# Transposing q and k by DMA instead of on TensorE, from tile 14 of 36 on, with six output staging buffers and fewer weight buffers

## The chip, the cores and the metric

The kernel runs on one core of a Trainium2 chip. The time is the device time of that core in microseconds, the median of several executions. A profiled execution gives the trace. A difference under about 0.2% can hardly be told from none.

The engines that matter: TensorE (PE) multiplies matrices and also transposes, VectorE (DVE) and ScalarE (ACT) do elementwise work and empty PSUM, GpSimd (POOL) issues the loads here, and SyncE (SP) issues the output stores. Each engine works through its own queue in order.

## The reference

Sliding-window causal attention with a linear bias (ALiBi) over 8 batches, 8 heads, 576 positions and head dimension 64, then a gated feed-forward layer over the 4608 tokens.

```python
scores = scale * np.matmul(q, k.transpose(0, 1, 3, 2))        # [8, 8, 576, 576]
mask = (rel >= 0) & (rel < 128)                               # rel = i - j
scores = np.where(mask, scores + slopes * -abs(rel), -1e9)
attn = softmax(scores)
x = np.matmul(attn, v)                                        # to [4608, 512]
g = x @ w_gate                                                # [512, 1536]
out = (g * sigmoid(g) * (x @ w_val)) @ w_out                  # [4608, 512], float32
```

## The kernel before

**Tiles.** The 4608 tokens are cut into 36 tiles of 128, numbered 0 to 35 in the order of loading (the code calls the number `rank`). Two batches make a pair `s` of nine tiles: four full tiles of each batch, and tile 4 of the pair (ranks 4, 13, 22, 31), which combines the last 64 rows of both. `source` gives where a tile lies in HBM.

**Loads.** POOL loads q, k and v of a tile (`qn`, `kn`, `va`) and turns float32 into float16 on the way. `qn` and `kn` have four buffers each, `va` has fourteen places.

**Transposes.** The scores need q and k with the head dimension on the partitions: `qT` and `kT`, one buffer for a pair `s`, two buffers in all. `transposed` makes them: four 128x128 transposes on PE into a PSUM tile `pt` (line 162) and one copy by DVE into `qT` or `kT` (line 163). That is eight transposes and two copies for a tile.

**Attention.** Unit `i` of 36 takes 128 keys. `scores` multiplies them with 256 queries into PSUM (`ps`, line 221; `psc`, line 192, for the combined tile), ACT takes the exponent (`exr`, `exrc`), DVE multiplies with a constant mask that holds the bias (`ex`; `exl` for the last full tile of a batch, which the combined tile needs again; `exc` for the combined tile). `weighted` multiplies with v (`av`) and divides by the sum, which gives `x`. `x_transposed` brings x onto the partitions (`px`, `xT`). The PSUM pool `ps_a` with four banks serves `pt`, `ps`, `psc`, `av` and `px`.

**Feed-forward.** Nine blocks `n` of 512 tokens. `gate_val` makes `pg` (line 302) and `pv` (line 312), ACT and DVE make `hT` from them; `project` multiplies with `w_out` into `po` (line 326), ACT scales it into the staging buffer `osb` (line 330), and SP stores that (line 332). The projection of block n-1 runs between the parts of block n.

**Order.** One function emits both: after every step of the feed-forward, as many attention steps follow as a rate (`RATE`) asks for, and at least those that the next block needs. `attention` transposes what unit i+1 needs, computes its scores, then the weighted sum of unit i, then it loads tile i+7 and calls `ahead`. `ahead` transposes what unit i+4 needs, but only where the tile's number reaches `QK_DMA_FROM`; at 99 it does nothing. A scheduler then orders the instructions within each engine, so that the written order is not the order on the queues, and it sets the waits.

Of the kernel before, what the change touches and what calls it, by code (L numbers as in the profile page):

```python
# [10 lines left out]
FP16 = mybir.dt.float16  # L11
# [3 lines left out]

P = 128
WIN = 128
QK_DMA_FROM = 99
X_DMA_FROM = 99
FIRST = 4  # L20
RATE = 5.2
# [20 lines left out]
def kernel(  # L42
# [11 lines left out]
    B, H, S, D = q.shape  # L54
# [46 lines left out]
    epool = ctx.enter_context(tc.tile_pool(name="ep", bufs=3))  # L101
# [1 line left out]
    bpool = ctx.enter_context(tc.tile_pool(name="bp", bufs=3))  # L103
    hpool = ctx.enter_context(tc.tile_pool(name="hp", bufs=18))
    supool = ctx.enter_context(tc.tile_pool(name="sup", bufs=4))
    opool = ctx.enter_context(tc.tile_pool(name="op", bufs=3))
    ps_f = ctx.enter_context(tc.tile_pool(name="ps_f", bufs=3, space=PSUM))
    ps_a = ctx.enter_context(tc.tile_pool(name="ps_a", bufs=4, space=PSUM))

# [15 lines left out]
    def col_of(p):  # L125
        return p if p < 4 else (p + 1 if p < 8 else 4)
# [38 lines left out]
    def transposes(rank):  # L165
        s, c = divmod(rank, 9)
        if s not in qTs:
            qTs[s] = tpool.tile([P, 4, 9 * P], FP16, name="qT", tag="qT")
            kTs[s] = tpool.tile([P, 4, 9 * P], FP16, name="kT", tag="kT")
        if rank >= QK_DMA_FROM:  # L170
            cols = slice(c * P, (c + 1) * P)
# [9 lines left out]
    def scores(i):  # L181

        s, p = units[i]
        c = col_of(p)
        kcols = slice(c * P, (c + 1) * P)
        kT, qT = kTs[s], qTs[s]
        if p == 8:
            banks = [ps_a.tile([P, 4, P], FP32, name="psc", tag="a") for _ in range(2)]
            for j in range(4):
                for par in range(2):  # L190
                    rows = slice(64 * par, 64 * par + 64)
                    nc.tensor.matmul(banks[par][:, j, :], kT[rows, j, kcols], qT[rows, j, kcols],
                                     start=(j == 0), stop=(j == 3))
            er = epool.tile([P, H, P], FP16, name="exrc", tag="exrc", bufs=2)
            e = epool.tile([P, H, P], FP16, name="exc", tag="exc", bufs=2)
            ex[(s, p)] = e

            er4 = er.rearrange("k (a par b) q -> k a par b q", a=2, par=2)

            def act(par):  # L200
                nc.scalar.activation(er4[:, :, par], banks[par].rearrange("k (a b) q -> k a b q", a=2),
                                     AF.Exp, scale=scale)

            return [[lambda: act(0)],
                    [lambda: act(1), lambda: nc.vector.tensor_mul(e, er, com)], [], []]

        banks = []
        for q4 in range(2):
            two = [ps_a.tile([P, 2, 256], FP32, name="ps", tag="a") for _ in range(2)]
            banks.append(two)  # L210
            for j in range(2):
                pair = 2 * q4 + j
                if p == 7:
                    parts = [(0, slice(8 * P, 9 * P)), (P, slice(4 * P, 5 * P))]
                else:
                    parts = [(0, slice(c * P, (c + 2) * P))]
                for n, (o, cols) in enumerate(parts):
                    w = cols.stop - cols.start
                    for par in range(2):
                        rows = slice(64 * par, 64 * par + 64)  # L220
                        nc.tensor.matmul(two[par][:, j, o:o + w], kT[rows, pair, kcols],  # L221
                                         qT[rows, pair, cols],
                                         start=(j == 0 and n == 0),
                                         stop=(j == 1 and n == len(parts) - 1))
        er = epool.tile([P, H, 256], FP16, name="exr", tag="exr", bufs=2)
        if p in (3, 7):
            e = epool.tile([P, H, 256], FP16, name="exl", tag="exl", bufs=3)
        else:
            e = epool.tile([P, H, 256], FP16, name="ex", tag="ex", bufs=3)
        ex[(s, p)] = e  # L230
        m = lo if p == 3 else hi if p == 7 else reg

        def act(q4, par):
            o = 4 * q4 + 2 * par
            nc.scalar.activation(er[:, o:o + 2, :], banks[q4][par], AF.Exp, scale=scale)  # L235

        def mul(q4):
            o = slice(4 * q4, 4 * q4 + 4)
            nc.vector.tensor_mul(e[:, o, :], er[:, o, :], m[:, o, :])  # L239

        return [[lambda: act(0, 0)], [lambda: act(0, 1), lambda: mul(0)],
                [lambda: act(1, 0)], [lambda: act(1, 1), lambda: mul(1)]]
# [112 lines left out]
    def transposes_to(r):  # L355
        nonlocal done_t
        while done_t <= min(r, NR - 1):
            transposes(done_t)
            done_t += 1

    def ahead(i):

        r = min(need_rank[min(i + 4, last)], loaded - 1)
        if r >= QK_DMA_FROM:
            transposes_to(r)

    def attention():

        transposes_to(need_rank[0])
        for steps in scores(0):  # L370
            for f in steps:
                f()
        yield 0
        for i in range(last + 1):
            after = [[], [], [], []]
            if i < last and i != FIRST - 1:
                transposes_to(need_rank[i + 1])
                after = scores(i + 1)
            if i == 1:
                make_lo()  # L380
            if i == 5:
                make_hi()
                make_com()
            for fs in after:
                for f in fs:
                    f()
                yield i
            weighted(i)
            yield i
            if i >= FIRST:  # L390
                loads_to(i + 7)
                ahead(i)
            yield i
            x_transposed(i)
            yield i
            yield i + 1
            if i == FIRST - 1:

                transposes_to(need_rank[i + 1])
                for fs in scores(i + 1):  # L400
                    for f in fs:
                        f()
                    yield i + 1
# [79 lines left out]
```

## Time and profile before

| | |
|---|---|
| median of 3 runs | 387.88 us (387.79 to 388.63) |
| profiled execution | 388.84 us, span 387.1 us |
| granted TensorE clock | 0.998 |
| PE transposes of q and k | 288 matmuls (line 162), 72 copies on DVE (line 163) |
| output stores | 40 on SP's queue, 2.0 us to landing for a full tile |
| loads of a q, k or v tile | 4.8, 4.5 and 5.9 us to landing (median) |

In the lines of the profile a group's row reads: line, engine, operation, output<-inputs, shapes, count | busy us, mean ns of one | idle time of that engine just before, and what ended it. A row of the timeline begins with the start and the length in us. A row by stage gives start:end, length, and for each engine the busy us and the number of instructions, then the granted clock, the DMA share and GB/s. A wait's row gives who waited for whom: us in total, times, the longest. A row of an issue ends with the median us from issue to landing. SPq and POOLq are those engines' own issuing queues.

### The profile page before, as it was taken

Reading aid. Unit: us, or ns where it says so; the run is one execution under the profiler, and the core shown is the slowest. Engines: PE = TensorE matmul, PEld = TensorE weight load, DVE = VectorE, ACT = ScalarE, POOL = GpSimd, SP = SyncE. Lnnn points to the kernel's source line nnn. Section 1 sums busy time; section 2 is a strip of 40 time slices with the busy share of each in tenths; the row PEclk is TensorE's granted clock in tenths of the full one; section 3 lists DMA queues with packets and bytes.
Section 4 is the critical chain, followed back from the end, with each engine's and each line's share of the span. In section 5 each row is a group of like instructions: output and inputs, shape, how many; then the busy total and the mean of one; then the engine's idle time right before and its main releaser. Section 6 shows DMA issues by size and latency. Waiting matters only on the chain.

```text
span 387.1 us, 6587 instructions
## 1 busy us (share of the span) xinstructions
PE 365.6 (94%) x2592; PEld 181.1 (47%) x2592; DVE 250.2 (65%) x515; ACT 173.8 (45%) x317; POOL 108.7 (28%) x134
## 2 busy tenths in 40 slices
PE   1889899999999999999999999999999999999994
PEld 1454345545545455554454544545454444444441
DVE  3765798757976598558865687668843752753540
ACT  1552474455544554545654456454633323332321
POOL 8966648842422055225200531000000000000000
PEclk9999999999999999999999999999999999999999
DMA  9999999999897369599441956310011001001013
GB/s 143 141 156 189 181 180 132 142 118 84 54 69 96 68 42 95 84 83 96 32 51 56 93 31 42 69 52 6 0 56 54 2 27 54 29 20 62 30 27 82
DMA packets 123872, 29.31 MB, mean 76 GB/s; under 512 B 114496, under 2 KB 119104, under 8 KB 123840
## 3 DMA queue, kind: packets, MB, share of 16 engines
q0 software_dynamic: 118304, 18.88, 73.5%
q1 hardware_dynamic: 5536, 10.00, 7.7%
q8 instruction: 20, 0.33, 0.3%
q14 instruction: 12, 0.10, 0.1%
HBM read 38.31 MB, written 9.44 MB: 123 GB/s over the span
## 4 chain that ended last, share of the span: by engine, by line
PE 77%; DMA 6%; DVE 6%; POOL 5%; ACT 4%; issue 2%; DVEq 0%; POOLq 0%; ACTq 0%
PE po L326 22%; PE pv L312 21%; PE pg L302 21%; PE ps L221 4%; PE pt L162 3%; PE av L266 3%; DMA qn<-in_q_dram 3%; DMA wg_sb<-in_moe_w_gate_dram 3%; ACT exr L235 2%; PE px L291 2%; DVE hT L314 2%; POOL qn L149 1%; POOL kn L149 1%; POOL va L143 1%; DVE ex L239 1%
## 5 line engine op out<-in xcount | busy, mean ns | idle before, releaser
L312 PE MATMUL pv<-xT,wv_sb 128*128 128x512 f16 x432 | 116.4, 382 | 0.0
L302 PE MATMUL pg<-xT,wg_sb 128*128 128x512 f16 x432 | 114.0, 381 | 0.7 <-ACT xT L292 0.7
L307 DVE SCALAR_TENSOR_TENSOR uu<-tt,pg 128x512 f16<-128x512 f16 x108 | 74.0, 685 | 59.4 <-ACT tt L305 58.8
L326 PE MATMUL po<-wo_sb,hT 128*128 128x512 f16 x432 | 104.0, 379 | 0.0
L305 ACT ACTIVATE tt<-pg 128x512 f16<-128x512 f32 x108 | 64.9, 601 | 80.2 <-PE pg L302 79.9
L235 ACT ACTIVATE exr<-ps 128x512 f16<-128x512 f32 x128 | 67.7, 608 | 38.4 <-PE ps L221 38.4
L314 DVE TENSOR_TENSOR hT<-uu,pv 128x512 f16<-128x512 f16 x108 | 74.0, 685 | 12.5 <-PE pv L312 5.5
L302 PEld LDWEIGHTS <-wg_sb 128*128 128x128 f16 x432 | 40.6, 98 | 43.8 <-issue 3.7
L312 PEld LDWEIGHTS <-wv_sb 128*128 128x128 f16 x432 | 40.1, 98 | 43.5 <-issue 4.4
L326 PEld LDWEIGHTS <-hT 128*128 128x128 f16 x432 | 39.9, 98 | 42.9 <-issue 1.9
L149 POOL DMA_DIRECT2D qn<-in_q_dram x40 | 34.0, 853 | 62.7 <-PE pt L162 59.0
L330 ACT ACTIVATE osb<-po 128x512 f32<-128x512 f32 x36 | 21.7, 603 | 57.2 <-PE po L326 50.7
L143 POOL DMA_DIRECT2D va<-in_v_dram x40 | 34.0, 856 | 35.0 <-PE av L266 29.7
L149 POOL DMA_DIRECT2D kn<-in_k_dram x40 | 34.1, 856 | 29.6 <-PE pt L162 23.3
L239 DVE TENSOR_TENSOR ex<-exr,m_reg 128x1024 f16<-128x1024 f16 x48 | 32.6, 687 | 12.4 <-ACT exr L235 12.1
L292 ACT COPY xT<-px 128x512 f16<-128x512 f16 x36 | 21.0, 584 | 31.5 <-PE px L291 31.5
L269 DVE TENSOR_TENSOR x<-av,rec 128x256 f16<-128x256 f32 x72 | 29.1, 420 | 0.7
L221 PE MATMUL ps<-qT,kT 64*128 64x256 f16 (+1 forms) x288 | 28.8, 274 | 0.7 <-DVE kT L163 0.3
L291 PE MATMUL px<-idm,x 128*128 128x128 f16 x144 | 19.8, 230 | 4.1 <-DVE x L269 3.8
L266 PEld LDWEIGHTS <-ex 128*128 128x128 f16 x384 | 18.8, 101 | 8.3 <-issue 2.2
L163 DVE COPY qT<-pt 128x512 f16<-128x512 f16 x36 | 14.9, 421 | 12.0 <-PE pt L162 11.8
L221 PEld LDWEIGHTS <-kT 64*128 64x128 f16 x288 | 13.4, 96 | 19.4 <-issue 15.2
(35 smaller groups left out, 166.9 us busy)
## 6 DMA issues: line engine op xcount, KB each, us to landing
out_dram<-osb SPq DMA_DIRECT2D x32, 256.0 KB, 2.0
kn<-in_k_dram POOLq DMA_DIRECT2D x32, 128.0 KB, 4.5
qn<-in_q_dram POOLq DMA_DIRECT2D x32, 128.0 KB, 4.8
va<-in_v_dram POOLq DMA_DIRECT2D x32, 128.0 KB, 5.9
wo_sb<-in_moe_w_out_dram POOLq DMA_DIRECT2D x2, 768.0 KB, 11.8
wg_sb<-in_moe_w_gate_dram POOLq DMA_DIRECT2D x2, 512.0 KB, 10.3
wv_sb<-in_moe_w_val_dram POOLq DMA_DIRECT2D x2, 512.0 KB, 11.8
out_dram<-osb SPq DMA_DIRECT2D x8, 128.0 KB, 2.4
```

What stands on the lines that cost most here:

```text
L143: nc.gpsimd.dma_start(va[rank][p0:p1, :, 0:D], src)
L149: nc.gpsimd.dma_start(t_[p0:p1], src)
L221: nc.tensor.matmul(two[par][:, j, o:o + w], kT[rows, pair, kcols], qT[rows, pair, cols], start=(j == 0 and n == 0), stop=(j == 1 and n == ...
L235: nc.scalar.activation(er[:, o:o + 2, :], banks[q4][par], AF.Exp, scale=scale)
L239: nc.vector.tensor_mul(e[:, o, :], er[:, o, :], m[:, o, :])
L266: nc.tensor.matmul(av[:, j, :], w, val, start=(n == 0), stop=(n == len(todo) - 1))
L302: nc.tensor.matmul(pg, wg_sb[:, kb, ms], xT[n][:, kb, :], start=(kb == 0), stop=(kb == NKB - 1))
L305: nc.scalar.activation(tt, pg, AF.Tanh, scale=0.5)
L307: nc.vector.scalar_tensor_tensor(out=uu, in0=tt, scalar=1.0, in1=pg, op0=ALU.add, op1=ALU.mult)
L312: nc.tensor.matmul(pv, wv_sb[:, kb, ms], xT[n][:, kb, :], start=(kb == 0), stop=(kb == NKB - 1))
L314: nc.vector.tensor_mul(hT[(n, m)], uu, pv)
L326: nc.tensor.matmul(po, hT[(n, m)][:, j * P:(j + 1) * P], wo_sb[:, m, :], start=(m == 0), stop=(m == NMB - 1))
```

## The change

From tile 14 on, `transposes` sends `qn` and `kn` through a transposing DMA on SP's queue, from SBUF to SBUF, straight into `qT` and `kT`; no PE transpose, no PSUM tile and no DVE copy are left for these 22 tiles. `ahead` becomes active with it, so that those transfers are written three units before the scores need them. Staging buffers `osb` go from three to six; `exrc` and `exc` from two to one, `exl` from three to two.

```diff
-QK_DMA_FROM = 99
+QK_DMA_FROM = 14
...
-    opool = ctx.enter_context(tc.tile_pool(name="op", bufs=3))
+    opool = ctx.enter_context(tc.tile_pool(name="op", bufs=6))
...
-            er = epool.tile([P, H, P], FP16, name="exrc", tag="exrc", bufs=2)
-            e = epool.tile([P, H, P], FP16, name="exc", tag="exc", bufs=2)
+            er = epool.tile([P, H, P], FP16, name="exrc", tag="exrc", bufs=1)
+            e = epool.tile([P, H, P], FP16, name="exc", tag="exc", bufs=1)
...
-            e = epool.tile([P, H, 256], FP16, name="exl", tag="exl", bufs=3)
+            e = epool.tile([P, H, 256], FP16, name="exl", tag="exl", bufs=2)
```

The line that takes effect with it stands in `transposes` already:

```python
nc.sync.dma_start_transpose(dst[:, :, cols], t_.rearrange("p h d -> p (h d)"))
```

On SP the queue held two constants and then only the stores of the output. Its start before (numbers behind a name tell the buffers' uses apart):

```order
L67 DMA idm_58<-ident16 128x128
L70 DMA m_reg_60<-mask_reg 128x2048
L332 DMA out_0_dram<-osb_1019 128x512
L332 DMA out_0_dram<-osb_1125 128x512
L332 DMA out_0_dram<-osb_1191 128x512
```

And now, behind the same two constants: `qn_921` and `kn_919` are tile 14, `1069` and `1067` tile 15, `1173` and `1171` tile 16, `1301` and `1299` tile 17, `1417` tile 18.

```order
L173 DMA_TRANSPOSE qT_962<-qn_921 128x4x128
L173 DMA_TRANSPOSE kT_963<-kn_919 128x4x128
L332 DMA out_0_dram<-osb_1019 128x512
L173 DMA_TRANSPOSE qT_962<-qn_1069 128x4x128
L173 DMA_TRANSPOSE kT_963<-kn_1067 128x4x128
L332 DMA out_0_dram<-osb_1125 128x512
L173 DMA_TRANSPOSE kT_963<-kn_1171 128x4x128
L173 DMA_TRANSPOSE qT_962<-qn_1173 128x4x128
L173 DMA_TRANSPOSE qT_962<-qn_1301 128x4x128
L173 DMA_TRANSPOSE kT_963<-kn_1299 128x4x128
L173 DMA_TRANSPOSE qT_1733<-qn_1417 128x4x128
L332 DMA out_0_dram<-osb_1219 128x512
```

The four stores of the first block now stand among the transposes of tiles 14 to 21, the four of the second block behind those of tile 26, and all transposes stand ahead of the third block's stores.

On POOL, from the load of tile 14 on, q and k came one tile at a time between the loads of v:

```order
L149 DMA qn_921<-in_q_dram 128x8x64
L149 DMA kn_919<-in_k_dram 128x8x64
L143 DMA va1_100<-in_v_dram 128x8x64
L143 DMA va2_102<-in_v_dram 128x8x64
L143 DMA va4_106<-in_v_dram 64x8x64 x2
L149 DMA qn_1069<-in_q_dram 128x8x64
L149 DMA kn_1067<-in_k_dram 128x8x64
L149 DMA qn_1173<-in_q_dram 128x8x64
L149 DMA kn_1171<-in_k_dram 128x8x64
L143 DMA va4_106<-in_v_dram 128x8x64
```

Now q and k of several tiles follow each other, and v comes behind them:

```order
L149 DMA qn_921<-in_q_dram 128x8x64
L149 DMA kn_919<-in_k_dram 128x8x64
L143 DMA va1_100<-in_v_dram 128x8x64
L149 DMA qn_1069<-in_q_dram 128x8x64
L143 DMA va2_102<-in_v_dram 128x8x64
L149 DMA kn_1067<-in_k_dram 128x8x64
L143 DMA va4_106<-in_v_dram 64x8x64 x2
L149 DMA kn_1171<-in_k_dram 128x8x64
L149 DMA qn_1173<-in_q_dram 128x8x64
L149 DMA qn_1301<-in_q_dram 128x8x64
L149 DMA kn_1299<-in_k_dram 128x8x64
L149 DMA qn_1417<-in_q_dram 128x8x64
```

The loads moved ahead of v's; what they wait for is now the transfer that empties their buffer, not PE.

On DVE, at the place of tiles 14 and 15, four copies stood between the feed-forward's products (`uu`, `hT`) before:

```order
L307 SCALAR_TENSOR_TENSOR uu_1434<-tt_1432,pg_1427 128x512
L163 COPY qT_962<-pt_1442 128x4x128
L314 TENSOR_TENSOR hT_1426<-uu_1434,pv_1436 128x512
L163 COPY kT_963<-pt_1448 128x4x128
L163 COPY qT_962<-pt_1454 128x4x128
L163 COPY kT_963<-pt_1460 128x4x128
L307 SCALAR_TENSOR_TENSOR uu_1489<-tt_1487,pg_1482 128x512
```

Now the product of the mask and the exponents (`ex`) follows at once:

```order
L307 SCALAR_TENSOR_TENSOR uu_1442<-tt_1440,pg_1435 128x512
L314 TENSOR_TENSOR hT_1434<-uu_1442,pv_1444 128x512
L239 TENSOR_TENSOR ex_1463<-exr_1462,m_reg_60 128x1024 x2
L307 SCALAR_TENSOR_TENSOR uu_1473<-tt_1471,pg_1466 128x512
L314 TENSOR_TENSOR hT_1465<-uu_1473,pv_1478 128x512
```

The copies are gone, and the scores of the unit that needs tiles 14 and 15 moved to the place where the transposes of tile 14 stood.

## The prediction

> **What bounds the kernel now.** I read the page's busy table first, then the same table by stage, then the chain of waits and single stretches of the timeline.
>
> ```profile
> PE 365.6 (94%) x2592; PEld 181.1 (47%) x2592; DVE 250.2 (65%) x515; ACT 173.8 (45%) x317; POOL 108.7 (28%) x134
> PE 77%; DMA 6%; DVE 6%; POOL 5%; ACT 4%; issue 2%; DVEq 0%; POOLq 0%; ACTq 0%
> ...
> core 0: us, PE busy (x) PEld busy (x) DVE busy (x) ACT busy (x) POOL busy (x), PEclk, DMA share, GB/s
> 0.00:90.00 90.00, 75.06 (x592) 39.04 (x593) 60.31 (x141) 41.44 (x77) 61.80 (x79) 1.00 2.03 151
> 90.00:270.00 180.00, 178.81 (x1410) 90.30 (x1408) 131.50 (x281) 94.73 (x176) 46.88 (x56) 1.00 0.66 63
> 270.00:387.10 117.10, 111.75 (x594) 51.73 (x592) 58.37 (x95) 37.58 (x65) 0.00 (x0) 0.99 0.12 37
> ```
>
> TensorE (PE) is 94% busy and makes 77% of the chain. The stages say where: in the first 90 us it idles 15 us, from 90 to 270 us only 1.2 us out of 180. In that middle stretch VectorE (DVE) has 48 us free and ScalarE (ACT) 85 us. So there, and only there, an instruction taken from PE's queue shortens the run by the time it held the queue. The clock is full (1.00), so no throttle will take the gain back.
>
> A busy PE counts overlapping matmuls, so the price of a transpose must come from start times, not from its mean duration:
>
> ```profile
> L162 PE MATMUL pt<-idm,kn 128*128 128x128 f16 x144 | 15.4, 234 | 6.8 <-DMA kn<-in_k_dram 6.7
> L162 PE MATMUL pt<-idm,qn 128*128 128x128 f16 x144 | 15.2, 234 | 3.2 <-DMA qn<-in_q_dram 3.2
> L163 DVE COPY kT<-pt 128x512 f16<-128x512 f16 x36 | 15.0, 418 | 5.1 <-PE pt L162 5.0
> ...
> 213.60 0.39 PE L162 MATMUL pt<-idm,kn 128*128 128x128 f16 x4
> 213.83 0.61 PE L162 MATMUL pt<-idm,qn 128*128 128x128 f16 x8
> 214.27 0.39 PE L162 MATMUL pt<-idm,kn 128*128 128x128 f16 x4
> 214.50 0.81 PE L326 MATMUL po<-wo_sb,hT 128*128 128x512 f16 x3
> ```
>
> The sixteen transposes of tiles 27 and 28 start at 213.60 and the next matmul starts at 214.50: 0.90 us for 16, 0.056 us each, not the 0.234 us of the group's mean.
>
> **The change, part by part.** *Transposes removed.* Tiles 14 to 35 are 22 tiles, with four transposes for q and four for k: 176 transposes. At 0.90 us per 16 this is 11 x 0.90 = 9.9 us of PE's queue. All of it lies in the full stretch, since the first removed ones and the last ones are these:
>
> ```profile
> 101.40 0.39 PE L162 MATMUL pt<-idm,qn 128*128 128x128 f16 x4
> ...
> 102.30 1.03 PE L302 MATMUL pg<-xT,wg_sb 128*128 128x512 f16 x4
> 103.16 0.59 PE L312 MATMUL pv<-xT,wv_sb 128*128 128x512 f16 x2
> 103.69 0.61 PE L221 MATMUL ps<-qT,kT 64*128 64x256 f16 x8
> ...
> 262.93 0.39 PE L162 MATMUL pt<-idm,qn 128*128 128x128 f16 x4
> 263.15 0.39 PE L162 MATMUL pt<-idm,kn 128*128 128x128 f16 x4
> 263.37 0.59 PE L302 MATMUL pg<-xT,wg_sb 128*128 128x512 f16 x2
> ```
>
> Here the Trainium skill speaks against the change. Its page "VectorE: DVE Perf Modes", section "The three transpose paths", gives a 128x128 transpose 390 ns on TensorE and 1309 ns by DMA, and its rules for kernel authors prefer TensorE where PSUM will do as the target. By its 390 ns the removed work would be 176 x 0.39 = 68.6 us, an estimate; the rows above show 56 ns of queue per transpose, and they decide.
>
> *Copies removed.* 44 PSUM copies of 0.418 us leave DVE: 18.4 us. I count them as nothing: DVE's 48 us of idle time in the same stretch already cover them.
>
> *Order on PE.* In the changed program the transposes of tiles 12 and 13 (still on PE) stand earlier, and the score matmuls break into the gate and value matmuls less often: counted over the whole order, 19 such breaks instead of 29. A break costs about 0.10 us: two `pv` from 103.16 would end by pitch at 103.59 (0.86 us per four, as from 102.30 to 103.16), and `ps` starts at 103.69. Ten fewer are worth at most 1.0 us. Eight scores in a row can also wait longer for ACT to empty their banks, which may take as much back. I take -0.4 us, between 0 and -1.0.
>
> *DMA transposes added.* 44 transfers of 128x512 fp16 (128 KB) go on SP's queue. The trace has none, so the price is bounded by the nearest transfers:
>
> ```profile
> out_dram<-osb SPq DMA_DIRECT2D x32, 256.0 KB, 2.0
> kn<-in_k_dram POOLq DMA_DIRECT2D x32, 128.0 KB, 4.5
> qn<-in_q_dram POOLq DMA_DIRECT2D x32, 128.0 KB, 4.8
> va<-in_v_dram POOLq DMA_DIRECT2D x32, 128.0 KB, 5.9
> L332 SPq DMA_DIRECT2D out_dram<-osb x40: 332/332/588, 73.1 to 383.0; - x40
> ```
>
> 2.0 us from below (an output store on the same queue, in long rows) and 5.9 us from above (a 128 KB load in 256-byte pieces). A transpose also has to cut its tile in small pieces, so it is nearer to the `kn` load: I take 4 us from issue to landing. Whether it holds the queue that long, or overlaps its successor as stores and loads do, is what decides; the issue itself, 0.33 us for a store, is no limit for 44.
>
> When are they needed? In the changed order the scores that use tiles 14 and 15 stand on PE just where the transposes of tile 14 stood, with the same instructions ahead, so they are due at 101.40. The loads that feed them:
>
> ```profile
> 71.83 0.89 POOL L149 DMA_DIRECT2D qn<-in_q_dram  x1 [0.50 <-PE ps L221]
> 73.26 0.88 POOL L149 DMA_DIRECT2D kn<-in_k_dram  x1 [0.54 <-PE av L266]
> ```
>
> These are tile 14. Its q lands near 71.83 + 4.8 = 76.6. With T for one DMA transpose, its q is transposed at 76.6 + T. The changed program loads q of tile 15 into the buffer that this frees: landed at 76.6 + T + 4.8, transposed at 81.4 + 2T. That meets 101.40 as long as T is under 10 us; 4 us leaves 12 us. Behind that, transposes go up to four tiles ahead of the loads, one tile being due every 7.3 us ((262.93 - 101.40) / 22), while four buffers turn over one tile in (4.8 + 4) / 4 = 2.2 us. So they stay hidden behind PE's work.
>
> *Loads moved.* Loads of q and k no longer wait for PE (before, POOL waited 82 us for it):
>
> ```profile
> POOL qn L149 <- PE pt L162: 59.0, 13, 8.2
> POOL kn L149 <- PE pt L162: 23.3, 2, 21.1
> ...
> 132.84 0.40 PE L192 MATMUL psc<-qT,kT 64*128 64x128 f16 x8
> ...
> 202.01 0.65 PE L266 MATMUL av<-va,ex 128*128 128x65 f16 x16
> ```
>
> They now wait for SP's transposes, and run far ahead. Loads of v that stand behind them on POOL come later than before, but the latest in order (tiles 26 and 27) only wait for tile 31's transposes, which stand on SP behind the transposes of tile 27; these wait for the last scores of the second pair (`psc`, 132.84) to leave a `qT` and `kT` buffer free. Two rounds of a load and a transpose later (2 x 9 us) they land, near 152 us; v of tile 26 is used at 202.01. Hidden.
>
> *Stores moved.* On SP the stores stand behind transposes that wait for loads:
>
> ```profile
> 83.89 0.60 ACT L330 ACTIVATE osb<-po 128x512 f32<-128x512 f32 x1 [2.92 <-PE po L326]
> 90.44 0.60 ACT L330 ACTIVATE osb<-po 128x512 f32<-128x512 f32 x1 [2.30 <-issue]
> 115.03 0.60 ACT L330 ACTIVATE osb<-po 128x512 f32<-128x512 f32 x1 [0.29 <-PE po L326]
> ```
>
> The store of the 83.89 us tile waits for tile 17 (81.4 + 2T + 4.8 = 94 us at T = 4), a delay of 10 us. Four outputs per block and a pause of 24 us to the next block: six staging buffers hold them all. The third to sixth buffer are worth nothing else, since the tail's stores took 2 us each.
>
> *Single buffers.* The combined tile comes once in nine units (its scores at 132.84 here), its weights are used some units later and long before the next one; two instead of three long-lived `exl` likewise. Nothing.
>
> Sum: 388.84 us of the profiled execution (span 387.1, 1.7 us around it) - 9.9 - 0.4 = 378.5. The median of the runs shown, 387.88, is 0.96 us below that execution, so **377.6 us**.
>
> **Rivals.** *The transposes queue one behind the other (slower).* If each holds the transfer path for its whole time P, 44 in a row from 76.6 must end by the time tile 35 is due, 262.93 - 9.4 = 253.5: P under 4.0 us. At the `kn` load's 4.5 us they end at 76.6 + 198 = 274.6, PE waits 21 us in all, and the time is 377.6 + 21 = 399 us. It costs all of the gain from P = 4.25 us on (10.3 us late). For it: 4 us is inside my own bounds. Against it: the loads land in 4.5 to 4.8 us yet POOL issues them every 0.9 us, so this chip's transfers overlap.
> The Trainium skill's pages take both sides. Four of the 1309 ns blocks of "VectorE: DVE Perf Modes" ("The three transpose paths") would be 5.2 us per transfer, an estimate by which the end is at 76.6 + 230 = 306 us, 53 us late, near 430 us. "DMA: Bandwidth & Descriptors", section "Latency and other measured facts", has 261 GB/s for DMA transposes, 0.5 us for 128 KB, an estimate by which they never queue. No run here shows either.
>
> *Late only at the start.*
>
> ```profile
> 118.05 0.39 PE L162 MATMUL pt<-idm,qn 128*128 128x128 f16 x4
> ...
> DMA to landing us min/median/max: 2.9/4.8/12.0
> ```
>
> T between 10 and 13 us, overlapping: tile 15 is up to 6 us late, the following ones little more. At T = 12 it is 81.4 + 24 - 101.4 = 4.0 us, and tile 17, loaded after it, 86.2 + 36 - 122 = 0.2 us more (due at 118.05 by its own transposes before, with the 4 us): 382 us. For it: a load can take 12.0 us to land, as the row shows (min, median, max). Against it: the DMA share falls from 2.03 to 0.66 after 90 us.
>
> *No change.* Something else takes over where PE was: the scores' banks, since the same stretch keeps ACT and DVE in the loop of scores, exponent and product, and the order on PE is new. It would have to add 9 us of waits to a stretch that has 1.2: 387.9 us.
>
> **How the numbers follow.** Gain as summed: 0.80, its own range 375.5 to 380 (the ends: all 1.0 us of breaks and the 1.2 us of idle gone; or 2 us of new waits). Late at the start: 0.06 (0.05 of it still faster, 0.01 slower). Queueing: 0.10, slower. No change: 0.04 (0.03 within the bound, 0.01 slower). A measurement of this kernel tells 0.2% (0.8 us) from nothing. Faster 0.85, same 0.03, slower 0.12. The range runs from 375.5 to 384, which takes in the late start and leaves out the queueing and no change.
>
> **What would show it.** Right: 112 `pt` matmuls instead of 288, PE's busy time near 356 us, PE idle under 3 us between 90 and 260 us, DMA transposes landing in 2 to 6 us, and scores that never wait for a transfer. Wrong: PE waiting for transfers at the scores (first tile 15, near 101 us; a wait that grows from tile to tile would be queueing), ACT's `osb` waiting for a store, or a weighted sum waiting for a v load.

## The result, and the profile after

The changed kernel takes 375.38 us (median of 4 runs, 374.97 to 377.44) where the kernel before takes 388.09 us in the same comparison. The ratio is 0.9682, with a 95% interval of 0.9644 to 0.9719. The forecast was 377.6 us, between 375.5 and 384: faster, as forecast, and by 12.7 us where 10.3 were summed up. That is the lower end of the range and no more: as a time 375.38 us lies 0.1 us under it, and as a ratio (0.9682 of the 387.88 us that the forecast started from) it is 375.5 us.

The busy table, the stages (start:end, length, busy us per engine, granted clock, DMA share, GB/s) and the transfers of the kernel after:

```profile
span 373.8 us, 6285 instructions
PE 351.6 (94%) x2416; PEld 170.4 (46%) x2416; DVE 235.9 (63%) x471; ACT 173.4 (46%) x317; POOL 108.6 (29%) x134
0.00:90.00 90.00, 74.86 (x602) 39.58 (x603) 60.91 (x144) 41.62 (x78) 61.89 (x79) 1.00 1.90 155
90.00:260.00 170.00, 167.66 (x1250) 80.56 (x1249) 118.21 (x238) 95.69 (x179) 46.71 (x56) 1.00 1.08 99
260.00:373.80 113.80, 109.11 (x568) 50.23 (x565) 56.79 (x91) 36.12 (x62) 0.00 (x0) 1.00 0.12 38
...
kn<-in_k_dram POOLq DMA_DIRECT2D x32, 128.0 KB, 7.0
qn<-in_q_dram POOLq DMA_DIRECT2D x32, 128.0 KB, 7.1
...
L173 SPq DMA_TRANSPOSE qT<-qn x22: 1189/1223/2181, 76.4 to 167.5; - x22
DMA to landing us min/median/max: 2.6/6.6/8.5
```

TensorE (PE) has 2592 - 2416 = 176 matmuls less and is nearly as full as before: 2.3 us of idle time in the 170 us of the middle stage, where it had 1.2 in 180. The DMA share of that stage went from 0.66 to 1.08. The last row group is the new work: SP is held 1.22 us (median, in ns: min/median/max) by a DMA transpose of q, which lands 6.6 us after its issue, and the last one starts at 167.5 us, long before its tile was transposed on PE (262.93 us).

PE's waits in the kernel after (engine, line, what it waited for: us in total, times, longest):

```profile
PE pt L162 <- DMA kn<-in_k_dram: 7.5, 2, 6.3
PE px L291 <- DVE x L269: 3.0, 6, 0.8
PE pt L162 <- DMA qn<-in_q_dram: 2.6, 3, 1.9
PE pv L312 <- DVE uu L307: 1.0, 3, 0.4
```

No wait of the scores (`ps`) for a DMA transpose is among them. The waits for loads of q and k belong to the start, whose transposes stayed on PE. The wait of `pv` for `uu`, a product that VectorE makes, is new, and it counts below.

**Where the 12.7 us came from.** The order on PE up to the first projection is the same in both kernels, so the stretch from the first to the last `po` matmul leaves out the start, which differs by a microsecond or two from profile to profile. In the rows it stands behind the durations, "first to last":

```profile
L326 PE MATMUL po<-wo_sb,hT x432: 377/379/390, 63.5 to 381.4; 128*128 128x512 f16 x144
```

That is before, 317.9 us. And after, 305.8 us:

```profile
L326 PE MATMUL po<-wo_sb,hT x432: 377/379/390, 63.0 to 368.8; 128*128 128x512 f16 x144
```

12.1 us less in this stretch. Where they lie can be summed from the starts of PE's matmuls. The time from one start to the next belongs to the first of the two. Where the next is of another kind and comes later than the usual pitch (216 ns behind a matmul with 512 columns, 56 behind a transpose, 30 behind `av`), the rest is the gap ahead of that next one.

| PE, from the first to the last `po`, us | before | after | difference |
|---|---|---|---|
| transposes of q and k (216 before, 40 after) | 12.2 | 2.4 | -9.9 |
| scores with the gap ahead of them | 21.5 | 17.1 | -4.4 |
| gaps ahead of `pv` | 0.3 | 2.3 | +2.0 |
| all else | 283.9 | 284.1 | +0.2 |
| sum | 317.9 | 305.8 | -12.1 |

The removed transposes are the 9.9 us that were summed up. The scores became 4.4 us cheaper because they break into other work less often. How dear a break is shows in a unit whose scores are split (before) and one whose scores are whole (after), both among the matmuls of `pv`:

```profile
149.12 0.59 PE L312 MATMUL pv<-xT,wv_sb 128*128 128x512 f16 x2
149.65 0.61 PE L221 MATMUL ps<-qT,kT 64*128 64x256 f16 x6
150.19 0.39 PE L312 MATMUL pv<-xT,wv_sb 128*128 128x512 f16 x1
150.58 0.38 PE L221 MATMUL ps<-qT,kT 64*128 64x256 f16 x2
150.89 0.39 PE L312 MATMUL pv<-xT,wv_sb 128*128 128x512 f16 x1
151.12 1.03 PE L302 MATMUL pg<-xT,wg_sb 128*128 128x512 f16 x4
```

```profile
99.48 1.03 PE L312 MATMUL pv<-xT,wv_sb 128*128 128x512 f16 x4
100.44 0.61 PE L221 MATMUL ps<-qT,kT 64*128 64x256 f16 x8
100.99 0.82 PE L302 MATMUL pg<-xT,wg_sb 128*128 128x512 f16 x3
```

Four `pv` and eight `ps` take 2.00 us (149.12 to 151.12) with two entries into the scores, and 1.51 us (99.48 to 100.99) with one. So a further break costs 0.49 us there, and not 0.10 us. Counted over PE's whole queue, the scores are entered 48 times before and 39 times after (all kinds of work ahead of them, where the prediction counted only the gate's and value's). 4.4 us over 9 entries is 0.49 us each, as in these rows.

About half of it is lost again ahead of `pv`, in six places between 104 and 255 us. In all six, ScalarE takes the four exponents (`exr`) of eight scores without a break, the feed-forward's `tt` comes only behind them, and `uu` on VectorE, for which `pv` waits, comes late with it. One of the six, from the timeline of all engines:

```profile
214.35 0.61 PE L221 MATMUL ps<-qT,kT 64*128 64x256 f16 x8
214.78 2.06 ACT L235 ACTIVATE exr<-ps 128x512 f16<-128x512 f32 x4 [0.59 <-PE ps L221]
...
216.71 0.63 ACT L305 ACTIVATE tt<-pg 128x512 f16<-128x512 f32 x1
...
218.22 1.02 PE L312 MATMUL pv<-xT,wv_sb 128*128 128x512 f16 x4 [0.30 <-DVE uu L307]
```

The row of waits above has only 1.0 us of it, in three places, since it counts longer idle times behind the modelled end of the matmul ahead. With this loss taken off, an entry fewer is worth about a quarter of a microsecond (2.2 us over 9).

### The profile page after: what moved, and what is told of

The parts are those of the page before. It is cut to its first block, busy times and chain, and to the rows that moved or that the text cites. A ratio compares the mean times of both kernels' runs of the same rounds, so it can differ in the third digit from the quotient of the medians.

```text
span 373.8 us, 6285 instructions
## 1 busy us (share of the span) xinstructions
PE 351.6 (94%) x2416; PEld 170.4 (46%) x2416; DVE 235.9 (63%) x471; ACT 173.4 (46%) x317; POOL 108.6 (29%) x134
## 4 chain that ended last, share of the span: by engine, by line
PE 72%; DVE 8%; DMA 7%; ACT 6%; POOL 4%; issue 2%; DVEq 0%; POOLq 0%
PE po L326 24%; PE pv L312 19%; PE pg L302 18%; ACT exr L235 5%; DMA qn<-in_q_dram 3%; PE ps L221 3%; PE av L266 3%; DMA wg_sb<-in_moe_w_gate_dram 3%; PE px L291 2%; DVE uu L307 2%; DVE hT L314 2%; DVE ex L239 2%; DMA kn<-in_k_dram 1%; POOL qn L149 1%; DVE x L269 1%
## 5 line engine op out<-in xcount | busy, mean ns | idle before, releaser
L312 PE MATMUL pv<-xT,wv_sb 128*128 128x512 f16 x432 | 113.5, 380 | 1.3 <-DVE uu L307 1.0
L302 PE MATMUL pg<-xT,wg_sb 128*128 128x512 f16 x432 | 112.4, 381 | 0.7 <-DMA va<-in_v_dram 0.7
L239 DVE TENSOR_TENSOR ex<-exr,m_reg 128x1024 f16<-128x1024 f16 x48 | 33.0, 689 | 19.0 <-ACT exr L235 18.9
L221 PE MATMUL ps<-qT,kT 64*128 64x256 f16 (+1 forms) x288 | 24.9, 274 | 0.3
L266 PE MATMUL av<-va,ex 128*128 128x65 f16 x384 | 20.9, 199 | 0.8 <-ACT exr L235 0.6
L291 PEld LDWEIGHTS <-x 128*128 128x128 f16 x144 | 10.1, 99 | 20.5 <-DVE x L269 17.0
```

The costliest lines, as they stand in the source:

```text
L266: nc.tensor.matmul(av[:, j, :], w, val, start=(n == 0), stop=(n == len(todo) - 1))
L291: nc.tensor.transpose(pt[:, kb, :], x[:, kb * P:(kb + 1) * P], idm)
L302: nc.tensor.matmul(pg, wg_sb[:, kb, ms], xT[n][:, kb, :], start=(kb == 0), stop=(kb == NKB - 1))
L312: nc.tensor.matmul(pv, wv_sb[:, kb, ms], xT[n][:, kb, :], start=(kb == 0), stop=(kb == NKB - 1))
```

## The experiments

The theory after the result: the time is PE's queue, 0.056 us for each transpose and, with the loss ahead of `pv` taken off, about a quarter of a microsecond for each entry into the scores, and the entries fell because the PSUM copies no longer hold banks of the pool that the scores use. Rivals: the staging buffers; VectorE's relief; the waits for loads. Differences below are of medians. The kernel before had 388.1 to 388.6 us in the comparisons, so such a difference is known to about half a microsecond; where a microsecond counts, it is of the stretch from the first to the last `po`.

**Buffers alone.** All transposes on PE, the changed pools kept.

```diff
-QK_DMA_FROM = 14
+QK_DMA_FROM = 99
```

> All transposes stay on TensorE; only the staging buffers (six) and the smaller weight pools of the change are kept. Theory (the gain is TensorE time: 9.9 us of transposes and about 2.8 us of fewer breaks of scores into other work): 388.1 us, within 0.8 us of before. Rival (part of the gain comes from more staging buffers): 2 to 3 us faster than before, 385 to 386 us.

388.67 us, ratio to before 1.0005 (0.9990 to 1.0019). The buffers alone do nothing.

**Three staging buffers.** The change without its six buffers for the output.

```diff
-    opool = ctx.enter_context(tc.tile_pool(name="op", bufs=6))
+    opool = ctx.enter_context(tc.tile_pool(name="op", bufs=3))
```

> The change with three staging buffers instead of six. Prediction's step (stores are late but the buffers beyond the third only matter for the second block): in the trace of the changed kernel the four stores of the second block issue at 129 to 131 us and land at 136 to 139, while their tiles are scaled from about 111 to 128 us; with three buffers the fourth needs the first one's, free at 136 us, so ScalarE would stand about 8 us and TensorE wait behind it: 380 to 384 us. Rival (six buffers are not needed): 375.4 us, within 1 us of the changed kernel.

384.32 us, 0.9892 (0.9874 to 0.9910): 8.9 us of the gain are lost. ScalarE's scaling of the second block's four outputs and SP's queue in that kernel:

```profile
123.89 0.63 ACT L330 ACTIVATE osb<-po 128x512 f32<-128x512 f32 x1
135.95 0.60 ACT L330 ACTIVATE osb<-po 128x512 f32<-128x512 f32 x1 [10.94 <-DMA out_dram<-osb]
...
127.86 1.19 SPq L173 DMA_TRANSPOSE qT<-qn  x1
129.14 7.77 SPq L332 DMA_DIRECT2D out_dram<-osb  x4
...
138.30 1.86 PE L312 MATMUL pv<-xT,wv_sb 128*128 128x512 f16 x4 [6.84 <-DVE uu L307]
```

The stores stand behind the transposes of tiles 22 to 26 until 129.14 us. The fourth output finds no buffer, ScalarE stands 10.94 us for a store, and PE waits 6.84 us behind the work queued on ScalarE. Behind this wait PE is slow for some microseconds: the four `pv` at 138.30 take 1.86 us where four take 1.03 elsewhere. The stage shows the granted clock at half:

```profile
138.30:142.00 3.70, 3.70 (x14) 1.46 (x14) 2.57 (x4) 0.79 (x3) 1.10 (x2) 0.50 2.02 195
```

By the starts of the matmuls that is another 2 us. So the six buffers are worth nothing alone and 8.9 us with the DMA transposes: the cover for stores that are late.

**PE's transposes back, without copies.** The data come by DMA; PE transposes a constant at the old places, and nobody reads the result.

```diff
+    extra = 14
+
+    def extra_to(r):
+        nonlocal extra
+        while extra <= min(r, NR - 1):
+            for _ in range(2):
+                pt = ps_a.tile([P, 4, P], FP16, name="pt", tag="a")
+                for j in range(4):
+                    nc.tensor.transpose(pt[:, j, :], reg[:, j, 0:P], idm)
+            extra += 1
...
             if i < last and i != FIRST - 1:
                 transposes_to(need_rank[i + 1])
+                extra_to(need_rank[i + 1])
```

> The DMA transposes stay, and TensorE does 176 transposes of a constant again at the places where it transposed q and k before; they go to PSUM and nobody reads them, so no copies on VectorE and no waits for loads come back. Theory: 176 x 0.056 = 9.9 us on top of the changed kernel, about 385.2 us, since the order of the scores stays that of the changed kernel (38 breaks into scores against 48 before). Rival (the transposes cost their whole difference, 12.7 us, through their interruptions of the queue): 388 us. Rival (VectorE's copies and the waits for loads were the larger part): 378 to 381 us.

385.41 us, 0.9917 (0.9888 to 0.9947): 10.0 us over the changed kernel, 0.057 us for each of 176. The runs spread over 3.9 us, so the closer figure is that of the trace: between the first and the last `po` the transposes take 12.2 us instead of 2.4, 0.056 us each. The price by start times holds.

**VectorE's time back, first try.** 44 copies of a constant in SBUF on VectorE, in `extra_to` in place of the transposes.

```diff
+                nc.vector.tensor_copy(spare, reg[:, 0:4, :].rearrange("p h q -> p (h q)"))
```

> The change, with 44 copies of a constant on VectorE at the places of the former PSUM copies, 128x1024 fp16 each, about 0.42 us, 18 us in all; their result is used by nobody. Theory (VectorE's idle time covers them): 375.4 us, within 1 us of the changed kernel. Rival (the gain beyond the transposes' own 9.9 us is VectorE's relief): 377.5 to 378.5 us.

378.72 us, 0.9742 (0.9725 to 0.9759). It looks like the rival, but the copies depended on nothing and were ordered to the front (10.6 to 81.3 us). By stage, the first row:

```profile
0.00:90.00 90.00, 72.20 (x572) 38.03 (x573) 75.86 (x181) 40.40 (x75) 62.44 (x78) 0.94 1.88 149
...
PE ps L221 <- DVE qT L163: 3.9, 3, 3.4
```

VectorE works 75.86 us in the first 90 instead of 60.91, and PE waits there for the copies of `qT`. That says nothing on the copies' old places; a run with copies at their place follows below.

**Each DMA transpose twice.**

```diff
                 nc.sync.dma_start_transpose(
                     dst[:, :, cols], t_.rearrange("p h d -> p (h d)"))
+                twin = opool.tile([P, 4, P], FP16, name="twin", tag="twin", bufs=4)
+                nc.sync.dma_start_transpose(twin, t_.rearrange("p h d -> p (h d)"))
```

> Each DMA transpose is issued a second time into a scratch tile that nobody reads: 88 transfers on SP's queue instead of 44. In the changed kernel SP is held 1.22 us by each, 54 us in all, and the last lands at 175 us while the scores need it near 250 us. Theory (the queue has room): the last lands near 200 us and the time stays at 375.4 us, at most 1.5 us more. Rival (the transfers are close to their limit, as a cost of 4 us each in a row would have it): 388 us or more.

387.52 us, 0.9975 (0.9954 to 0.9995): the forecast of no change was wrong by 12 us, though not for the rival's reason. The transposes still run ahead of the scores; it is the stores that come late:

```profile
ACT osb L332 <- DMA out_dram<-osb: 9.5, 1, 9.5
PE po L328 <- ACT osb L332: 8.5, 2, 8.0
...
L173 SPq DMA_TRANSPOSE qT<-qn x22: 1196/1261/2804, 76.9 to 209.2; - x22
DMA to landing us min/median/max: 2.4/5.3/8.3
```

The transposes end at 209 us instead of 168, and the stores behind them keep six buffers full: ScalarE waits 9.5 us for a store, PE 8.5 us for ScalarE. Twice as many transfers do not land later after their issue (5.3 us against 6.6). What is short is the place in SP's queue: its transposes are 118 of the 135 us between the first and the last.

**Transposes and copies back.** The copies of the constant's transposes come back too, on VectorE.

```diff
                     nc.tensor.transpose(pt[:, j, :], reg[:, j, 0:P], idm)
+                nc.vector.tensor_copy(opool.tile([P, 4, P], FP16, name="spare", tag="spare", bufs=2), pt)
```

> As the kernel with 176 constant transposes back on TensorE, and the 44 PSUM copies (128x512 fp16, about 0.42 us) of their results back on VectorE too, into scratch. The data still come by DMA. Theory (the part of the gain beyond the transposes' own 9.9 us comes from the copies' hold on PSUM banks, which splits the scores: 56 breaks into the scores on TensorE's queue against 38 without the copies): 388 to 390 us, 3 to 4 us above the kernel without copies. Rival (VectorE's copies are covered by its idle time, and the rest of the gain is the waits for loads): 385.4 us.

391.08 us, 1.0059 (1.0039 to 1.0078): 5.7 us above the kernel without the copies, and above before; 1 us more than the theory's range. The copies are not free.

**Short copies back.** The same with `pt[:, :, 0:4]`, sixteen elements a partition. By the trace such a copy takes 0.17 us, not 0.07; a full one takes 0.42 us on VectorE.

> As the one before, but each copy takes only 4 of 128 columns of each block (16 elements a partition), some 0.07 us: it frees the PSUM bank but hardly holds VectorE. TensorE's queue has 44 breaks into the scores. Theory (breaks, 0.28 us each): 38 to 44 is 1.7 us over the kernel without copies, about 387 us. Rival (VectorE's time): 385.4 us. Rival (banks held, whatever the order): 388 us or more, as with full copies.

385.98 us, 0.9930 (0.9911 to 0.9949): 0.6 us above the kernel without copies by the median, nearer to the rival's 385.4 us than to the theory's 387; the runs of the two kernels overlap. In the stretch of the projections it is 1.3 us (62.7 to 379.3 against 63.2 to 378.5), and the table below splits it.

**Copies by ScalarE.** The full copies, made by ScalarE instead of VectorE (`nc.scalar.copy`), 0.59 us each.

> As the kernel with the 176 constant transposes and 44 full PSUM copies back, but ScalarE makes the copies (about 0.58 us each) and VectorE none. TensorE's queue then has 68 breaks into the scores (56 with VectorE's copies, 38 without copies). Theory (a copy costs by holding a PSUM bank, over which the scores are split; whose time it takes does not matter): 391 us or more, by the order some 394 us. Rival (it is VectorE's time that was relieved): about 386 us, as with the short copies.

395.60 us, 1.0192 (1.0165 to 1.0220). VectorE does not do one of the added copies and the kernel is slower still: the copies' cost is not VectorE's time. ScalarE did have room, 111.4 us busy of 180 in the stage from 90 to 270 us:

```profile
90.00:270.00 180.00, 178.29 (x1352) 89.40 (x1349) 110.19 (x223) 111.40 (x211) 46.29 (x55) 1.00 1.06 94
...
L326 PE MATMUL po<-wo_sb,hT x432: 377/379/390, 62.9 to 388.3; 128*128 128x512 f16 x144
...
PE ps L221 <- ACT spare L376: 1.1, 6, 0.2
```

PE is 99% busy in it all the same: the cost lies inside its queue. The last row shows the bank at work: in six places the scores wait for a copy of ScalarE, whose result nobody reads, to leave its bank. Entries into the scores, the stretch from first to last `po`, and the two rows of the sum by starts that change most, for the kernels that do the same matmuls:

| kernel | entries into scores | stretch, us | over the one without copies | scores with the gap ahead, us | gaps ahead of `pv`, us |
|---|---|---|---|---|---|
| transposes back, no copies | 38 | 315.3 | | 16.5 | 2.9 |
| short copies | 44 | 316.6 | 1.3 for 6 more, 0.22 each | 20.1 | 0.7 |
| full copies, VectorE | 56 | 321.2 | 5.9 for 18 more, 0.33 each | 26.0 | 0.0 |
| full copies, ScalarE | 68 | 325.4 | 10.1 for 30 more, 0.34 each | 30.9 | 0.0 |

The scores themselves become 0.5 to 0.6 us dearer for each further entry (3.7, 9.5 and 14.4 us for 6, 18 and 30, their waits for the copies included), and up to 2.9 us come back where `pv` no longer waits. The longer a copy holds its PSUM bank, the more often the scores are split on PE's queue, and the time follows the splits. That the scheduler splits them because of the bank is inferred from this order.

**From tile 23 on.**

```diff
-QK_DMA_FROM = 14
+QK_DMA_FROM = 23
```

> DMA transposes from tile 23 on: 13 tiles instead of 22. Theory (TensorE time by tile, transposes and breaks counted over its order: 40 breaks): 7.8 us under before, 380.4 us. Rival (the tiles early in the run, where loads were waited for, carry the gain): 383 to 386 us. Rival (late tiles carry it): 376 to 378 us.

379.62 us, 0.9766 (0.9743 to 0.9789), 0.8 us from the forecast. Its stretch is 64.3 to 374.2, 8.0 us under before; 13 tiles at 0.45 us and 8 entries at 0.24 us make 7.8. The gain goes by the tile.

**VectorE's time back, at its place.** Copies of exponents in SBUF, two for each unit from 14 on; no PSUM bank is held. The trace has 38 of them, not 44, since the three combined units take another way through the code.

```diff
+    spare = consts.tile([P, 1024], FP16, name="spare")
...
             nc.vector.tensor_mul(e[:, o, :], er[:, o, :], m[:, o, :])
+            if i >= 14:
+                nc.vector.tensor_copy(spare, er[:, o, :].rearrange("p h q -> p (h q)"))
```

> The change with 44 copies on VectorE, 128x1024 fp16 of the exponents of units 14 to 35 in SBUF, 0.42 us each, 18 us in all, read by nobody: they stand where VectorE works on those units and hold no PSUM bank. Theory (not VectorE's time, but the PSUM bank that a copy holds, with the scores split over it, was the cost of the copies): about 1 us above the changed kernel, 376 to 377 us (42 breaks into scores on the queue against 39). Rival (VectorE's time itself): 379 us or more, as with the copies of PSUM, which cost 5.7 us.

378.52 us, 0.9735 (0.9707 to 0.9763): by the median 3.1 us over the changed kernel, between theory and rival, and the intervals of the two ratios overlap. The profile splits it:

```profile
L329 PE MATMUL po<-wo_sb,hT x432: 377/379/390, 64.9 to 372.7; 128*128 128x512 f16 x144
```

The first projection starts 1.9 us later than in the changed kernel, ahead of all added copies; the stretch behind it, 307.8 us, is 2.0 us longer. By the starts of the matmuls 1.8 of these 2.0 us are at the scores (18.9 against 17.1 us), which are entered three times more (42) and wait two more times for ScalarE to empty a bank; the gaps ahead of `pv`, where PE waits for VectorE, did not grow (2.2 against 2.3 us). So 16 us of VectorE's time back cost at most 2 us, and PE loses them at the scores, not in waits for VectorE.

**Two versions further on.** From tile 9 on, with seven staging buffers (`QK_DMA_FROM = 9`, `bufs=7`):

> DMA transposes from tile 9 on, five tiles more, with seven staging buffers. Theory (5 x 0.45 = 2.2 us of TensorE, 1.9 us by its order): 373.5 us. Rival (before 85 us the loads are not ahead of TensorE and land 7 to 12 us after their issue, so that the scores wait for the transfers, or a store behind them finds no buffer): 376 to 382 us.

380.88 us, 0.9791 (0.9764 to 0.9819): worse than from tile 14. PE's timeline names the wait, and the stages the clock behind it:

```profile
70.51 0.40 PE L221 MATMUL ps<-qT,kT 64*128 64x256 f16 x2 [5.40 <-DMA qT<-qn]
...
70.50:74.00 3.50, 3.49 (x13) 1.26 (x14) 0.69 (x1) 2.06 (x4) 2.93 (x4) 0.50 1.97 148
```

So early, the loads have little lead: q of tile 10 landed at 59.57 us, its transpose was issued at 60.36 and landed 10.0 us later. 5.40 us go in one wait of the scores, and the clock is at half behind it: the prediction's rival of a late start, at an earlier tile.

And the transposes of x by DMA from unit 24 on (`X_DMA_FROM = 24`, else as changed):

> The change, and the transposes of x go by DMA too from unit 24 on, when the transposes of q and k have all landed: 48 transposes of TensorE and 12 copies of ScalarE less. Theory (TensorE's queue is what counts, 3.9 us by its order): 371.5 us. Rival (x has no slack: it is made by VectorE just before the next block needs it, and a transfer takes 3 us or more where the copy took 0.6 us): TensorE waits up to 3 us at each of four blocks, 376 to 383 us.

372.67 us, 0.9585 (0.9561 to 0.9610): the best of all, by the medians 2.7 us under the changed kernel and 1.2 us over the theory; in the stretch 302.3 us, 3.5 us less. The transposes of q and k are over by then:

```profile
L287 SPq DMA_TRANSPOSE xT<-x x12: 1188/1190/2072, 198.9 to 277.2; - x12
DMA to landing us min/median/max: 2.4/2.4/3.2
```

PE has no wait for `xT` among its waits in this profile, so the rival's 3 us at each block fell.

## Why the prediction was right, and where it was off

**Transposes off PE, -9.9 us: right.** 176 at 0.056 us; putting them back cost 10.0 us by the medians, 9.8 us by the starts. The 390 ns that the Trainium skill's "VectorE: DVE Perf Modes" ("The three transpose paths") gives a TensorE transpose is seven times what one took from the queue here.

**Breaks, -0.4 us: mis-sized.** The prediction took 0.10 us for a break, from the gap ahead of the scores alone. The rows at 149.12 and 99.48 show what was left out, the gap behind the scores and the second start: 0.49 us each, 4.4 us in all. The loss that it set against them, ScalarE falling behind eight scores in a row, did come, but not at the scores' banks: `pv` waits 2.0 us more, for `uu`. What is left is 2.2 to 2.4 us instead of 0.4.

**The range: its lower end, and by luck.** The lower end was made of all 1.0 us of breaks and all 1.2 us of PE's idle time gone; with the 9.9 us these terms add up to 375.8 us, and 375.5 was written. The idle time of the middle stage did not go, it rose to 2.3 us. The mis-sized breaks made up for it, with 2.2 to 2.4 us where 1.0 and 1.2 were granted, so that the range reached far enough is luck.

**Copies off VectorE, nothing: nearly right for VectorE's time, wrong for the copy.** 16 us of copies back on VectorE that hold no bank cost at most 2.0 us in the stretch; the change had set 18.4 us free. But a copy is also the end of a PSUM bank's use. The step looked at the engine and not at the bank, and the sum had the bank's part only as the breaks; with the copies back the splits came back, 5.7 us on VectorE and 10.2 us on ScalarE over the kernel without them. The removed copies and the fewer breaks are one gain, not two.

**Price of a DMA transpose, 4 us: too low, and outside its bounds.** The median landing is 6.6 us, over the 5.9 us taken as the upper end; the loads beside them went from 4.8 to 7.1 us as well. It cost nothing because the condition was set apart from the price: under 10 us for tile 15. That tile's two transposes landed at 88.98 and 89.79 us and its scores began at 100.44, 10.7 us later, where the prediction had 12. PE never waited for a transfer at the scores.

**Issue on SP, no limit: only half right.** 1.22 us (median) instead of 0.33 us, 59 us in all; no limit for the transposes, but a delay for every store behind them. The prediction had the store of the third output at 94 us, and it went out late, at 98.83 us:

```profile
98.83 0.53 SPq L332 DMA_DIRECT2D out_dram<-osb  x1
```

That the six buffers hold the late stores was right. That they are close to the limit was not seen: with three the kernel loses 8.9 us, with twice the transfers 12.

**The queueing rival: ruled out as far as it went.** Transfers in flight overlap: 1.2 us apart on the queue, 6.6 us to landing. The prediction's estimate of 5.2 us for each, from the 1309 ns that the Trainium skill's "VectorE: DVE Perf Modes" ("The three transpose paths") gives a 128x128 block by DMA, does not hold here: with little else under way, four such blocks landed in 2.4 us (the transposes of x). The rival's break-even is a slip: at 4.25 us each the last would be 10.1 us late, not 10.3.

**The profile's marks.** 112 `pt` matmuls, 2.3 us of idle time (under 3 was said), no wait of PE for a transfer at the scores, none of `osb` for a store: as written. PE's busy time is 351.6 us, not 356, and the transposes' median to landing of 6.6 us lies outside the 2 to 6 us.

## What to carry to other kernels

On a full engine, price an instruction by start times, and price its interruption too: what stands ahead, what stands behind, and what the scores' or other short matmuls lose by being split. Then sum the starts by kind of work before and after: a net gain can hide a larger gain and a new wait. A copy that empties PSUM costs by the bank that it holds as well as by its engine's time, so an idle engine does not make it free. Where transfers of two kinds share one issuing queue, give the later kind buffers for the time that it stands in line, and ask which of both runs out first: here the output's staging buffers, not the transposed data.

## What the runs showed of the hardware

A DMA transpose of 128x512 fp16 within SBUF holds SP 1.19 to 1.22 us, where a store held it 0.33 us before and 0.53 to 0.58 us among the transposes. It lands after 2.4 us with little else under way, 6.6 us (median) beside the loads, and 10.0 us at most, in the start of the kernel from tile 9 on. Beside it the loads of q went from 4.8 to 7.1 us. More of them did not slow each other (5.3 us with 88).

A further entry into a group of scores (64*128 in the rows) between matmuls of 128*128 cost PE 0.5 to 0.6 us. Where PE stood 5.40, 6.84 and 8.03 us (from tile 9 on, three staging buffers, each transpose twice), the granted clock of the next 3.5, 3.7 and 3.8 us was 0.50. In some profiles the granted clock dipped in the first 90 us (0.94 in the row of the first try above). The start differed by up to 3 us between profiles (first projection at 61.8 to 64.9 us, that first try left out, whose order on PE is another), which is why the stretch behind it was compared.
